# A routing product placed after the token list, and no w_out conversion inside the first routing phase

## The chip, the core and the metric

The kernel runs on one core of one Trainium2 chip. The core has five engines, each with its own in-order instruction queue: PE (matrix products; its weight loads are shown as PEld), DVE (vector work), ACT (scalar activations, copies), POOL (simple vector work and the indexed DMAs) and SP (it issues most DMAs). An engine goes on to its next instruction only when the one in front has what it waits for. The metric is the device time of one execution in microseconds (us).

## What is computed

Three layers follow each other on 3072 tokens with 512 features.

```python
# 1 decayed linear attention, 4 batches x 8 heads x 768 steps x 64
state = gamma * state + k_t v_t^T ;  y_t = scale * q_t state
# 2 mixture of 8 experts: greedy by sorted logits, at most 384 tokens for each expert
logits = x @ w_gate
for (token, e) in order of falling logit: assign if token is free and count[e] < 384
out[tokens of e] = relu(x[tokens of e] @ w1[e]) @ w2[e]
# 3 dense layer
h = x @ w_in ;  out = softplus(h) @ w_out
```

`w_in` and `w_out` arrive as 64-bit floats and are turned into 32-bit ones on the chip with integer work ("conversion").

## The kernel before

**Stages.** The attention stage ends at about 113 us. Then routing finds the first expert and its 384 tokens (the first stage of routing, "phase 0", about 113 to 140 us), with PE kept busy by filler products (`hum`). After that eight experts are worked through, about 107 us each: layer 2 and layer 3 of one expert's tokens, in groups that `plan` lists. For expert i, `m1` and `m2` are the two products of layer 2 for one slice of 128 hidden features, `f1(i,f)` the product with slice f of `w_in` followed by the softplus, `f2(i,f)` the product with slice f of `w_out`, and `xt(i,g)` the transposition of 128 gathered token rows. Operands are split into a high and a low part, so each product is three matmuls. `f1` and `f2` alternate: f1(2), f2(0), f1(3), f2(1), ..., f1(15), f2(13). For expert 0 the three `xt` of expert 1 stand behind f2(9), f2(10) and f2(11).

**What a group gives each engine.** `emit` goes through the list. Before each group `weights` splits the weight slices needed four weighted groups later (ACT writes `whi`, DVE `wlo`). In f1(f) PE writes a PSUM tile `h`, of which there are three in rotation, shared with `m1` and `xt`; ACT makes `sp` from it with three instructions; DVE makes `gf`, which frees the tile; one f1 later ACT makes `gh` and DVE `gl`, which f2(f) needs for its last three matmuls. An `xt` tile is freed by DVE's `xl`.

**Conversion of w_out.** It is cut into 32 pieces and made during expert 0. Each piece takes two steps of `Conv`: a first (DVE, L286, writes `cB`) and a second (DVE, L288, writes `cA`; then POOL adds both, L289, and the next piece's ACT and POOL preparation is issued, POOL at L272 writing that piece's `cA`). So a piece's L288 waits for the POOL instruction L272 which stands behind the POOL addition of the piece before. From the fifth group of expert 0 on the groups do one and two steps by turns, so three in a pair of f1 and f2; and `split_w` first forces the pieces that its slice needs (`late.until`). Eight steps more are done inside phase 0, by `fill` in `start`.

**Routing.** `phase(i)` finds expert i and its tokens while the expert before is worked through. It is a generator; `emit` resumes it after most groups (a "turn"): after every group until the token list exists, after every second one then. In three levels of two comparisons DVE compares keys (`G`), PE counts, DVE decides (`left`, `ind`), PE sums (`upto`), DVE goes on. With the expert known ("expert"), PE and DVE compute positions (`scan`, `ohq` in three parts, `rh`) and twelve small products of `ohq` and `rh` give the token list `ix` ("list"). Then POOL gathers rows by `ix` (`fetch_x`: three indexed DMAs) for the next expert's `xt`. `taken` (14 DVE instructions, L638 to L657) marks the tokens that are gone and makes `rn`; the small product `rn` by `ones` (L606) gives the remaining places, `rem`. In phases 1 to 6 `taken` comes one turn ahead of that product, which stands directly ahead of the list's products; in phase 0 both come behind the list.

Of the kernel before, what the change touches and what calls it, by code (L numbers as in the profile page):

```python
# [52 lines left out]
class Attn:  # L53
# [143 lines left out]
    def hum(self, n):  # L197
        for _ in range(n):
            self.nc.tensor.matmul(self.ph, self.ones, self.ones, start=True, stop=True)
# [123 lines left out]
class Route:  # L323
# [148 lines left out]
        yield  # L472
        self.prepare(slice(c0, c1), 10, 2047, 0.0)

    def phase(self, i, slow=True, hum=lambda n: None, fill=lambda l: None):

        nc, N, E, w = self.nc, self.N, self.E, self.wp
        v = nc.vector
        T = lambda shape, dt, name, **k: w.tile(shape, dt, name=name, **k)
        gap = range  # L480
        last = i == E - 1
# [7 lines left out]
        for l, J in enumerate(() if last else LEVELS):  # L489
            if l:  # L490
                v.tensor_scalar(self.kx, self.bc(self.kp, N, 2), base, S, op0=OP.subtract, op1=OP.mult)
            top = None
            for fine in (0, 1):
                if i or l or fine:
                    thr = self.coarse[J]
                    if fine:
                        thr = T([128, 46], F16, "thr")[:, :J]
                        v.scalar_tensor_tensor(thr, top.to_broadcast([128, J]), J * S, self.jio[:, :J],
                                               op0=OP.mult, op1=OP.add)
                    cuts = (0, N) if slow else (0, N // 2, N - 4, N)  # L500
                    for c0, c1 in zip(cuts, cuts[1:]):
                        self.compare(c0, c1, thr, J, (64 if J > 32 else 32) if i else 46)
                    if l and not fine:
                        v.tensor_scalar(self.kf, self.kp, base, 3000.0 if l == 1 else 1.0, op0=OP.subtract,
                                        op1=OP.min if l == 1 else OP.add)
                    if l == 1 and fine:
                        self.prepare(all, 0, 1023, 4096.0)
                    if i and not l and not fine:
                        self.prepare(all, 10, 2047, 0.0)
                    fill(2 * l + fine)  # L510
                    for _ in gap(2):
                        yield
                ps = self.psum_tile()
                ind = self.ind
                if i:
                    self.count_many(ps, J)
                    self.reached(ps, J)
                else:
                    self.count(ps)
                    v.tensor_tensor(ind, ps[:, 0:E], self.r, op=OP.is_ge)  # L520
                for _ in gap(1 + (i > 1 or i + l > 1)):
                    yield
                f = 4096.0 if fine and l < 2 else 1.0
                nc.tensor.matmul(ps[:, 64:64 + E], self.upto[J, f], ind, start=True, stop=True)
                hum(9 if l == 2 and fine else 6 if fine else 5)
                k = T([128, 1], FT, "ksat", bufs=2)
                v.tensor_reduce(k, ps[:, 64:64 + E], axis=AX.X, op=OP.max)
                if fine:
                    base = T([128, 1], FT, "base")
                    v.scalar_tensor_tensor(base, top, J * f, k, op0=OP.mult, op1=OP.add)  # L530
                top = k
        inc = T([128, E], FT, "inc")
        if last:
# [12 lines left out]
            ps = self.psum_tile()  # L546
# [4 lines left out]
        g2 = T([128, 2, N], BF, "g2")  # L551
# [4 lines left out]
        es = T([128, 1], FT, "es")  # L556
# [23 lines left out]
        pE = pos[:, N:2 * N]  # L580
# [8 lines left out]
        for c0 in range(0, N, h):  # L589
# [3 lines left out]
            if c0 == 0:  # L593
# [2 lines left out]
                                self.cid[:, :, None, :].to_broadcast([128, N, 7, 2]), op=OP.mult)  # L596
                for _ in gap(1):
                    yield
        yield
        if slow:  # L600
            yield
            if not last:
                rn, oh = self.taken(T, pE, inc, g2, es)
            yield
            if not last:
                nc.tensor.matmul(ps[:, 136:136 + E], self.ones, rn, start=True, stop=True)  # L606
        for c in range(0, N, 2):
            nc.tensor.matmul(ps[:, 256:284], q[:, c:c + 2, :].rearrange("p n m -> p (n m)"),
                             rh[:, c:c + 2].rearrange("p n k a -> p (n k a)"), start=c == 0, stop=c == N - 2)
# [10 lines left out]
        yield "list"  # L620
        if last:
            return
        if not slow:
            rn, oh = self.taken(T, pE, inc, g2, es)
            for _ in gap(2):
                yield
            nc.tensor.matmul(ps[:, 136:136 + E], self.ones, rn, start=True, stop=True)
            hum(6)
# [35 lines left out]
class Ffn:  # L664
# [51 lines left out]
    def mm3(self, ps, wh, wl, ah, al, start, stop):  # L716
        nc = self.nc
        nc.tensor.matmul(ps, wh, ah, start=start, stop=False)  # L718
        nc.tensor.matmul(ps, wl, ah, start=False, stop=False)  # L719
        nc.tensor.matmul(ps, wh, al, start=False, stop=stop)  # L720
# [243 lines left out]
    def start(self, ps):  # L964


        hum = lambda n: self.hum(ps, n)
        self.keys = [g[3] for g in self.plan(self.R.E) if g[3]]
        self.loaded = self.done = self.listed = self.phase = 0
        self.gen = None  # L970
        def fill(level):
            for _ in range(2 if level > 1 else 0):
                self.late.step()

        self.late.ahead()
        hum(8)
        for mark in self.R.phase(0, False, hum, fill):
            self.marked(mark, 0)
            if mark == "expert":
                for k in self.keys[:3]:  # L980
                    self.load_raw(k)
                    self.loaded += 1
        self.weights(3)
# [95 lines left out]
```

## Time and profile before

| what | value |
|---|---|
| median of three runs | 1003.72 us (1001.87 to 1003.85) |
| the profiled execution | 1003.05 us, of which the span from first to last instruction is 1001.3 us |
| PE busy | 974.0 us, 97% of the span |
| DVE, ACT, POOL busy | 636.1 us (64%), 582.5 us (58%), 160.0 us (16%) |
| chain of work that ended last | PE 69%, issue 11%, DVE 10%, ACT 4%, DMA 4% of the span |

The span is 1.75 us shorter than the execution that it belongs to; what lies around it is taken as unchanged. PE is busy nearly everywhere, so the time can only change where PE stands still, where its clock is low, or where filler runs. The profile shows PE's granted clock as a share of full speed (1.00 is 2.4 GHz, 0.50 is 1.2 GHz).

### The profile page before, as it was taken

What the parts mean: (1) busy time and instruction counts of PE and PEld (TensorE: products, weight loads), DVE (VectorE), ACT (ScalarE), POOL (GpSimd) and SP (SyncE); (2) the same over time, 40 slices, a digit from 0 to 9 for tenths busy, and PEclk for the clock granted to TensorE, in tenths of its full rate; (3) what the DMA queues carried; (4) which work ended last, traced back from release to release, by engine and by line L of the source; (5) the groups of instructions that cost most, each with busy time, mean ns of one, the idle gap of its engine ahead of it and who ended that gap; (6) DMA issues with size and microseconds to landing.
All of it is one profiled execution on the core that took longest, in us unless ns stands there. A gap on an engine that the chain in (4) does not pass through costs nothing.

```text
span 1001.3 us, 17952 instructions
## 1 busy us (share of the span) xinstructions
PE 974.0 (97%) x6741; PEld 890.8 (89%) x6741; DVE 636.1 (64%) x1638; ACT 582.5 (58%) x1251; POOL 160.0 (16%) x184
## 2 busy tenths in 40 slices
PE   8999899979999999999999999999999999999997
PEld 7888789868998889998998899899989999999996
DVE  6899778787657655755566566655676654454442
ACT  5999525766446653665366645564466546653663
POOL 1655224556100110010101010101010100010001
PEclk9999879989999999999999999999999999999999
DMA  9999345223310123111411041103110340023000
GB/s 361 412 413 386 100 124 163 86 73 116 106 53 32 32 68 103 32 32 27 143 33 32 22 137 43 32 11 118 42 43 1 111 142 1 1 69 101 1 1 32
DMA packets 40599, 95.98 MB, mean 96 GB/s; under 512 B 5312, under 2 KB 5568, under 8 KB 40512
## 3 DMA queue, kind: packets, MB, share of 16 engines
q1 hardware_dynamic: 36528, 82.16, 24.3%
q0 software_dynamic: 3840, 12.59, 3.8%
q8 instruction: 53, 0.87, 0.4%
q14 instruction: 34, 0.28, 0.1%
q10 hardware_dynamic: 144, 0.09, 0.0%
HBM read 82.23 MB, written 12.58 MB: 95 GB/s over the span
## 4 chain that ended last, share of the span: by engine, by line
PE 69%; issue 11%; DVE 10%; ACT 4%; DMA 4%; POOL 1%; SPq 0%; POOLq 0%; ACTq 0%
PE h L726 10%; PE h L727 10%; PE h L729 10%; PE acc L836 6%; PE acc L837 6%; PE acc L841 6%; PE acc L718 4%; PE acc L719 4%; PE acc L720 4%; DMA qk_t<-in_qk_dram 3%; PE pX L184 1%; PE pA L131 1%; DVE gf L802 1%; PE pY L159 1%; PE h L750 1%
## 5 line engine op out<-in xcount | busy, mean ns | idle before, releaser
L802 DVE SCALAR_TENSOR_TENSOR gf<-h,sp 128x384 f32<-128x384 f32 x128 | 71.2, 556 | 171.5 <-ACT sp L793 171.3
L726 PE MATMUL h<-x2h,wih 128*128 128x384 f32 x512 | 176.8, 345 | 0.0
L727 PE MATMUL h<-x2h,wil 128*128 128x384 f32 x512 | 173.4, 339 | 0.0
L836 PE MATMUL acc<-whi,gh 128*128 128x512 f32 x384 | 154.0, 401 | 0.0
L837 PE MATMUL acc<-wlo,gh 128*128 128x512 f32 x384 | 152.0, 396 | 0.0
L791 ACT ACTIVATE sp<-h 128x384 f32<-128x384 f32 x128 | 62.7, 490 | 131.3 <-PE h L729 125.9
L841 PE MATMUL acc<-whi,gl 128*128 128x512 f32 x384 | 111.6, 397 | 0.0
L729 PE MATMUL h<-x2l,wih 128*128 128x384 f32 x512 | 111.0, 338 | 0.0
L710 ACT ACTIVATE h1h<-h 128x384 fp32r<-128x384 f32 x64 | 31.6, 493 | 132.6 <-PE h L729 96.6
L726 PEld LDWEIGHTS h<-x2h,wih 128*128 128x128 f32 x512 | 96.7, 189 | 3.2
L727 PEld LDWEIGHTS h<-x2h,wil 128*128 128x128 f32 x512 | 96.7, 189 | 3.2
L849 POOL DMA_INDIRECT out_dram<-rows,ix x24 | 24.6, 1023 | 438.3 <-ACT rows L847 434.9
L815 ACT ACTIVATE gh<-gf 128x384 fp32r<-128x384 f32 x128 | 67.3, 526 | 45.0 <-DVE gf L802 39.0
L704 DVE TENSOR_TENSOR wlo<-wraw,whi 128x512 fp32r<-128x512 f32 x128 | 86.7, 695 | 9.2 <-ACT whi L703 9.2
L729 PEld LDWEIGHTS h<-x2l,wih 128*128 128x128 f32 x512 | 91.6, 188 | 0.0
L711 DVE SCALAR_TENSOR_TENSOR h1l<-h,h1h 128x384 fp32r<-128x384 f32 x64 | 35.7, 558 | 87.4 <-ACT h1h L710 87.2
L703 ACT ACTIVATE whi<-wraw 128x512 fp32r<-128x512 f32 x128 | 77.3, 626 | 21.0 <-DMA wraw<-in_moe_w_dram 18.3
L704 DVE TENSOR_TENSOR wlo<-wol,whi 128x512 fp32r<-128x512 f32 x128 | 88.6, 698 | 0.9 <-ACT whi L703 0.8
L718 PE MATMUL acc<-h1h,whi 128*128 128x384 f32 x256 | 88.6, 346 | 0.0
L841 PEld LDWEIGHTS acc<-whi,gl 128*128 128x128 f32 x384 | 72.6, 189 | 17.5
L726 PE MATMUL h<-xh,whi 128*128 128x384 f32 x256 | 87.0, 340 | 0.5 <-ACT xh L754 0.5
L719 PE MATMUL acc<-h1h,wlo 128*128 128x384 f32 x256 | 86.3, 337 | 0.0
(197 smaller groups left out, 1931.5 us busy)
## 6 DMA issues: line engine op xcount, KB each, us to landing
wraw<-in_moe_w_dram SPq DMA_DIRECT2D x128, 256.0 KB, 2.8
qk_t<-in_qk_dram SPq DMA_DIRECT2D x24, 512.0 KB, 8.7
kv_t<-in_kv_dram SPq DMA_DIRECT2D x24, 512.0 KB, 8.7
raw<-in_moe_w_in_dram SPq DMA_DIRECT2D x16, 512.0 KB, 8.8
raw<-in_moe_w_out_dram SPq DMA_DIRECT2D x32, 256.0 KB, 2.9
xd<-xs SPq DMA_DIRECT2D x24, 256.0 KB, 7.9
rows<-xd,ix POOLq DMA_INDIRECT x24, 3.6
out_dram<-rows,ix POOLq DMA_INDIRECT x24, 3.7
```

Of the source, the lines that this page charges most:

```text
L703: nc.scalar.activation(hi, raw, AF.Copy)
L704: nc.vector.tensor_tensor(lo, raw, hi.bitcast(FT), op=OP.subtract)
L718: nc.tensor.matmul(ps, wh, ah, start=start, stop=False)
L719: nc.tensor.matmul(ps, wl, ah, start=False, stop=False)
L726: mm(ps, wh(d), ah[:, d], start=d == 0, stop=False)
L727: mm(ps, wl(d), ah[:, d], start=False, stop=False)
L729: mm(ps, wh(d), al[:, d], start=False, stop=d == 3)
L802: self.nc.vector.scalar_tensor_tensor(g, ps, 0.0, a, op0=OP.max, op1=OP.add)
L815: nc.scalar.activation(gh, g, AF.Copy)
L836: nc.tensor.matmul(ps, gh[:, s], wh, start=f == 0, stop=False)
L837: nc.tensor.matmul(ps, gh[:, s], wl, start=False, stop=False)
L841: nc.tensor.matmul(ps, gl[:, s], wh, start=False, stop=f == 15)
```

## The change

In phase 0 no conversion step is done any more: `fill` is gone, and the eight steps (four pieces) are done in expert 0 with the others. The number of steps for each group is as before; where the pieces for a slice are missing, `late.until` forces them.

In phases 1 and 2 `taken` and the product of `rn` move behind the list, with two turns from `taken` to the product, and the list's products stand alone; the number of turns ahead of the list is the same. In phases 3 to 6 (`joined`) the product stays directly ahead of the list's products, but `taken` comes three turns ahead of it, after three turns; the list is three turns later. Phase 1 waits one turn more between the first comparison of the third level and its count. The last phase does none of this.

```diff
-    def phase(self, i, slow=True, hum=lambda n: None, fill=lambda l: None):
+    def phase(self, i, slow=True, hum=lambda n: None):
...
-                    fill(2 * l + fine)
-                    for _ in gap(2):
+                    for _ in gap(2 + (i == 1 and l == 2 and not fine)):
                         yield
...
-        yield
-        if slow:
+        joined = i > 2 and not last
+        for _ in gap(1 + 2 * slow):
             yield
-            if not last:
-                rn, oh = self.taken(T, pE, inc, g2, es)
-            yield
-            if not last:
-                nc.tensor.matmul(ps[:, 136:136 + E], self.ones, rn, start=True, stop=True)
+        if joined:
+            rn, oh = self.taken(T, pE, inc, g2, es)
+            for _ in gap(3):
+                yield
+            nc.tensor.matmul(ps[:, 136:136 + E], self.ones, rn, start=True, stop=True)
...
-        if not slow:
+        if not joined:
             rn, oh = self.taken(T, pE, inc, g2, es)
             for _ in gap(2):
                 yield
...
-        def fill(level):
-            for _ in range(2 if level > 1 else 0):
-                self.late.step()
-
         self.late.ahead()
         hum(8)
-        for mark in self.R.phase(0, False, hum, fill):
+        for mark in self.R.phase(0, False, hum):
```

DVE in phase 0, third comparison, before: `kf` is the last of the comparison's work, `ind` the decision on what PE counted.

```order
L431 TENSOR_TENSOR G<-kx,coarse_81 128x184
L504 TENSOR_SCALAR kf<-kp,base 128x24
L286 SCALAR_TENSOR_TENSOR cB<-raw,cB 128x256
L288 TENSOR_SCALAR cA<-cA 128x256
L520 TENSOR_TENSOR ind<-pS,rem 128x8
L527 TENSOR_REDUCE ksat<-pS 128x1
```

And now:

```order
L431 TENSOR_TENSOR G<-kx,coarse_81 128x184
L504 TENSOR_SCALAR kf<-kp,base 128x24
L519 TENSOR_TENSOR ind<-pS,rem 128x8
L526 TENSOR_REDUCE ksat<-pS 128x1
L498 SCALAR_TENSOR_TENSOR thr<-ksat,jio 128x46
```

The two conversion instructions ahead of the decision are gone, in four places of phase 0.

PE in expert 0, phase 1, before: the `rn` product stands behind f1(9) (L726 to L729), and the list's products behind it.

```order
L727 MATMUL h<-x2h,wil 128x384
L729 MATMUL h<-x2l,wih 128x384 x4
L606 LDWEIGHTS ones
L606 MATMUL rt<-rn,ones 128x8
L608 LDWEIGHTS ohq
L608 MATMUL rt<-rh,ohq 128x28
```

Now the list's products stand behind f2(7), and the `rn` product behind f2(9) and xt(1,0), ahead of f1(12):

```order
L840 MATMUL acc_3004<-whi,gl 128x512
L840 MATMUL acc_3005<-whi,gl 128x512
L840 MATMUL acc_3006<-whi,gl 128x512
L749 MATMUL h<-identp,rows 128x128 x4
L626 LDWEIGHTS ones
L626 MATMUL rt<-rn,ones 128x8
L725 MATMUL h<-x2h,wih 128x384
```

The `rn` product has moved six groups back in PE's queue, the list's products one.

DVE in expert 0 now, from the list (in f2(7)) to the first instructions of `taken` (in f2(8)); `wol` is the converted w_out:

```order
L618 SCALAR_TENSOR_TENSOR ix<-i_3494 128x3
L286 SCALAR_TENSOR_TENSOR cB<-raw,cB 128x256
L703 TENSOR_TENSOR wlo<-wol,whi 128x512
L815 TENSOR_TENSOR gl<-gf,gh 128x384
L801 SCALAR_TENSOR_TENSOR gf<-h,sp 128x384
L288 TENSOR_SCALAR cA<-cA 128x256
L286 SCALAR_TENSOR_TENSOR cB<-raw,cB 128x256
L288 TENSOR_SCALAR cA<-cA 128x256
L637 SCALAR_TENSOR_TENSOR acc<-pos,mem 128x24
L639 TENSOR_TENSOR tin<-oe,inc 128x192
```

and POOL at the same place, with the gather for expert 1:

```order
L289 TENSOR_TENSOR wol<-cA,cB 128x256
L272 TENSOR_SCALAR cA<-cA 128x256
L738 DMA rows<-xd,ix 128x512 x3
L289 TENSOR_TENSOR wol<-cA,cB 128x256
L272 TENSOR_SCALAR cA<-cA 128x256
```

`taken` stands behind the list and behind two second steps (L288); the later of these needs POOL's L272 that stands behind the three gathering DMAs. From f1(7) to f1(11) a pair of f1 and f2 now holds four conversion steps, where it held three.

## Rows read from the trace of the kernel before

**Rows 1.** Waits of PE from 140 us on: total, times, longest (us).

```profile
PE rt L606 <- DVE rn L652: 8.4, 3, 6.8
PE rt L444 <- DVE G L431: 0.6, 1, 0.6
```

**Rows 2.** Windows: PE, PEld, DVE, ACT, POOL busy, PE clock, DMA share, GB/s.

```profile
110.00:140.00 30.00, 24.93 (x268) 22.68 (x265) 23.23 (x108) 7.30 (x16) 10.10 (x12) 0.66 0.37 110
130.00:140.00 10.00, 9.36 (x61) 8.81 (x61) 7.63 (x35) 1.90 (x3) 3.09 (x3) 0.62 0.43 120
215.00:232.00 17.00, 10.22 (x51) 8.97 (x50) 12.95 (x39) 5.89 (x14) 8.99 (x10) 0.70 0.26 82
```

**Rows 3.** Timeline of DVE in phase 0: start, length (us), instruction.

```profile
116.25 0.21 DVE L498 SCALAR_TENSOR_TENSOR thr<-ksat,jio 128x46 f16<-128x46 f32 x1
...
121.02 0.40 DVE L498 SCALAR_TENSOR_TENSOR thr<-ksat,jio 128x46 f16<-128x46 f32 x1
...
122.75 0.42 DVE L286 SCALAR_TENSOR_TENSOR cB<-raw,cB 128x256 int32<-128x256 int32 x1
123.09 0.29 DVE L288 TENSOR_SCALAR cA<-cA 128x256 int32<-128x256 int32 x1
123.29 0.16 DVE L520 TENSOR_TENSOR ind<-pS,rem 128x8 bf16<-128x8 f32 x1
```

**Rows 4.** Timeline of PE: phase 0's filler, ends of f1(6), f1(10), start of f1(14).

```profile
134.66 5.15 PE L962 MATMUL pA<-wih 128*128 128x256 f32 x30
...
203.57 0.87 PE L729 MATMUL h<-x2l,wih 128*128 128x384 f32 x4
...
223.97 0.17 PE L606 MATMUL rt<-rn,ones 128*128 128x8 bf16 x1 [6.78 <-DVE rn L652]
...
230.39 0.87 PE L729 MATMUL h<-x2l,wih 128*128 128x384 f32 x4
...
247.05 0.42 PE L726 MATMUL h<-x2h,wih 128*128 128x384 f32 x1
```

**Rows 5.** Timeline of DVE in expert 0, idle time and releaser in brackets.

```profile
204.21 0.16 DVE L527 TENSOR_REDUCE ksat<-rt 128x1 f32<-128x8 f32 x1
...
206.63 0.68 DVE L704 TENSOR_TENSOR wlo<-wol,whi 128x512 fp32r<-128x512 f32 x1
...
211.03 1.10 DVE L816 TENSOR_TENSOR gl<-gf,gh 128x384 fp32r<-128x384 f32 x1
...
212.84 0.24 DVE L574 TENSOR_TENSOR_SCAN scan<-ones,rt 128x48 f32<-128x48 bf16 x1
...
215.93 1.50 DVE L590 TENSOR_TENSOR ohq<-io,px 128x512 bf16<-128x512 bf16 x2
217.35 0.68 DVE L704 TENSOR_TENSOR wlo<-wol,whi 128x512 fp32r<-128x512 f32 x1
217.95 0.55 DVE L816 TENSOR_TENSOR gl<-gf,gh 128x384 fp32r<-128x384 f32 x1
218.42 0.54 DVE L802 SCALAR_TENSOR_TENSOR gf<-h,sp 128x384 f32<-128x384 f32 x1
...
220.93 0.29 DVE L288 TENSOR_SCALAR cA<-cA 128x256 int32<-128x256 int32 x1 [1.42 <-POOL cA L272]
221.14 0.18 DVE L638 SCALAR_TENSOR_TENSOR acc<-pos,mem 128x24 f32<-128x24 f32 x1
...
224.49 0.69 DVE L704 TENSOR_TENSOR wlo<-wol,whi 128x512 fp32r<-128x512 f32 x1
...
232.94 0.56 DVE L802 SCALAR_TENSOR_TENSOR gf<-h,sp 128x384 f32<-128x384 f32 x1 [3.12 <-ACT sp L793]
```

**Rows 6.** Timeline of POOL: the gather for expert 1 and the conversion behind it.

```profile
230.03 1.05 POOL L739 DMA_INDIRECT rows<-xd,ix  x1 [0.16 <-issue]
...
233.79 0.85 POOL L289 TENSOR_TENSOR wol<-cA,cB 128x256 int32<-128x256 int32 x1 [0.20 <-DVE cA L288]
234.61 0.85 POOL L272 TENSOR_SCALAR cA<-cA 128x256 f32<-128x256 f32 x1
```

## The prediction

> **What bounds the kernel now.** I read the waits of PE first. From 140 us to the tail PE waits for DVE at two kinds of place only: 8.4 us at the `rn` product, in three of its six occurrences, one of them 6.8 us, and 0.6 us once for a comparison `G` [rows 1]. Then the granted clock. The window 110 to 140 us has 0.66; at half speed that is (1 - 0.66) x 30 / 0.5 = 20.4 us at 1.2 GHz, in phase 0. The window 215 to 232 us has 0.70, so 10.2 us at 1.2 GHz, around the long `rn` wait [rows 2]. Everywhere else in the experts PE is busy at 2.4 GHz. So the change can act in phase 0, at the long stop in expert 0, and at the two short stops. The reader should see in [rows 5] why the long stop is there: DVE reaches `taken` at 221.14 and leaves it at 224.49, while PE, at the end of f1(9), has wanted its result since 223.97 - 6.78 = 217.2 [rows 4]. DVE is behind PE by three groups there, and this lag is not made by `taken` alone.
>
> **Phase 0, four pieces of conversion removed.** A first step takes 122.75 to 123.09, 0.34 us to the next start, a second one 0.20 [rows 3]. Four of each are 2.2 us of DVE, the most that can go. Not all of it is on the path: DVE decides on what PE has counted, and mostly the steps fit into PE's count. At 123.29 `ind` did start right behind L288, which I put at 0.35 us late. A small instruction that runs while POOL converts is longer: `thr` 0.40 us at 121.02 against 0.21 at 116.25 [rows 3]; I count five such places at 0.2. So DVE gives `ix` 0.35 + 5 x 0.2 = 1.4 us earlier; the ends are 0 and 2.2.
>
> Behind it PE runs 30 filler matmuls, 134.66 to 139.81 [rows 4], partly at half speed: the window 130 to 140 has 0.62, so the clock rose at about 137.6 [rows 2]. If it rises at the same moment, 1.4 us of earlier start are spent at half speed and give 0.7; if it rises with the filler, all 1.4. I take **-0.8 us**, from 0 to -1.6.
>
> SP, ACT and POOL lose the same four pieces there (four loads, ten ACT copies, the POOL halves); none of them ends last in phase 0, so that is worth nothing more.
>
> A rule bears on the five places. The trace has `thr` 0.19 us longer beside POOL. The Trainium skill, in "SBUF — State Buffer", section "SBUF: two separate sides", says that DVE and GpSimd share one port pair as an exclusive lock, and the later one blocks until the other's instruction is over. By it a hit costs up to the rest of a POOL instruction, and the trace agrees only in part: 0.19 us is less than that. By the rule's extreme the sum here would go to its end of 1.6.
>
> **The two short stops, phases 5 and 6.** 8.4 - 6.8 = 1.6 us [rows 1]. `taken` is 3.35 us of DVE (221.14 to 224.49) [rows 5] and had one turn ahead of the product; now it has three, at least 6 us. Worth **-1.6 us**. The list comes three turns later there, yet five or more groups ahead of the first `xt`; I cost that at nothing, and at up to +1 if DVE meets one of its bursts.
>
> **The long stop, expert 0.** Taking `rn` out of the way saves 6.8 us, and the low clock behind it: PE works again from 223.97, and by 230.39 four matmuls take 0.87 us as at 203.57 [rows 4], so it is at half speed for at most 6.4 us, some 3 lost. That would be -9.8 if DVE could follow. I follow DVE instead, turn by turn, up to the xt(1,1) tile, because f1(14) reuses its PSUM tile and can't start before DVE's `xl`.
>
> Where does DVE last wait for PE in the new order? In f1(6): phase 1's extra turn lets `expert` fall one group later, DVE has less ahead of it, and `gf` must wait for `sp`. PE ends f1(6) at 204.44 before [rows 4]; the 0.6 us for `G` is gone since that count stands one group later, so 203.8. From the end of f1(10), 231.26 [rows 4], to its `gf` at 232.94 [rows 5] are 1.7 us. So `gf` starts at 205.5, on the clock of the trace before (without the gain of phase 0).
>
> From there to the end of `xl` of xt(1,1) DVE has, at start-to-start prices of [rows 3, 5]:
> - 7 `gf` and 6 `gl` at 0.47 (217.95 to 218.42): 6.1
> - 7 `wlo` at 0.60 (217.35 to 217.95) and 2 `xl` of the same size: 5.4
> - 13 first steps at 0.34 and 14 second steps at 0.20: 7.2
> - routing: `expert` 2.42 (204.21 to 206.63), positions 2.55 (212.84 to 215.93 less one second and one first step), the rest of `ohq` 1.42, the list and `rem` some 1.5 (an estimate: eight instructions as short as `taken`'s), `taken` 3.35: 11.2
>
> Together 29.9 us. Then the waits inside DVE's own queue. A second step with little work since the one before waits for POOL: 1.42 at 220.93 [rows 5]. With four steps to a pair this comes in every pair in which no long routing piece stands between; in f2(5), f2(7), f2(9) and f2(10), 4 x 1.42 = 5.7. In f2(8) it is worse. POOL's L272 for that step stands behind the gather, 230.03 to 233.58 with its gaps, then 0.2 idle, L289 and L272 at 0.84 each [rows 6], 5.4 us in all. POOL starts it at about 227; DVE has 2 us of work of its own meanwhile and then stands for 3.7 us, with `taken` behind this wait. Last, instructions that meet POOL's are longer: `gl` 1.10 at 211.03 against 0.55 [rows 5]; half a microsecond in five places, 2.4. Sum: 205.5 + 29.9 + 5.7 + 3.7 + 2.4 = 247.2, against 247.05 when f1(14) starts now [rows 4].
>
> So in this stretch the gain is given back: `rn` is ready at about 235.5, PE stands there some 4.5 us behind xt(1,0), and again for both `xl`. **+0.2 us**; without lengthening beside POOL -2.2, with twice of it +2.6. Behind f1(14) conversion is over and DVE catches up.
>
> **Sum.** -0.8 - 1.6 + 0.2 = -2.2 us. Against the profiled execution, 1003.05, that is 1000.9; against the median of the runs shown, 1003.72, it is **1001.5**. The median lies 0.7 above the profiled one, and I give the forecast against it.
>
> **Rivals.**
> - *DVE follows.* The waits for POOL don't come, or not on the path: up to 5.7 + 3.7 us less on DVE's side. Then PE's own pace sets f1(14). From the end of f1(10) to f1(14) are seven groups and three `xt` in 15.8 us [rows 4], and f1(6) ends eight groups of some 2.1 us earlier: 203.8 + 16.8 + 15.8 = 236.4, even earlier than DVE allows. All of it gives **992**, half of it 997. For it: DVE's 29.9 us of work alone would let PE run on. Against it: in the trace L288 stood for POOL in just this order [rows 5].
> - *Slower: the clock.* PE stands 4.5 us at `rn`; before, 10.2 us at 1.2 GHz came with a stop of 6.8, and 20.4 us in phase 0 [rows 2]. From f1(12) on, a low stretch of L us costs L/2, less some 2.8 us for which PE would stand anyway for the two `xl`. 10.2 us cost 2.3 (1003.8), 20.4 us 7.4 (**1008.9**). It ends slower by over 0.2%, above 1005.7, once L passes 14 us. The Trainium skill ("TensorE: Matmul & The Clock Gate", "What's actually happening") says that half speed is PE's default state and activity releases it; the trace agrees, since the clock came back while PE worked. By the rule the new stop would bring a low stretch again, but one that ends with the work behind it: 1003.8 at most.
> - *No net change.* Phase 0 gives nothing because PE's filler and the gather set its end, and shifted turns in phases 3 to 6 meet new short stops: **1003.5**.
>
> **How the numbers follow.** A measurement of this kernel can tell about 0.2%, 2.0 us, from no change; so faster means below 1001.7 and the forecast lies right at that edge. Forecast 62%, its own range 999.5 to 1003.5, about half of it below the edge; DVE follows 13%; no net change 16%; the clock 9%, most of it slower. Faster 0.33 + 0.13 = 0.46; slower 0.07; same 0.47. The range leaves out most of the first rival and the worst of the second, which are under 2 in 10: 997.0 to 1004.5.
>
> **What would show it.** Right: the wait at L605/L626 in phase 1 still there, some 4 us, now behind xt(1,0) at about 230 to 235; DVE idle some 3.7 us ahead of the L288 in front of `taken`, released by POOL; no wait at the products of `rn` after 600 us; phase 0 shorter by under 1.5 us. Wrong: DVE without waits for POOL between 205 and 245, PE without a stop there, or a second long stretch at 0.50.

## The result, and the profile after

The changed kernel takes 1008.09 us (median of five runs, 1007.67 to 1010.95) where the kernel before takes 1002.69 (1001.87 to 1003.85). The ratio is 1.006, with a 95% interval of 1.0047 to 1.0074: slower by 0.6%, and outside the range of the prediction. The profiled execution has a span of 1006.3 us.

The waits of PE from 140 us on (total, times, longest, in us), which answer to [rows 1]:

```profile
PE acc L835 <- ACT gh L814: 5.1, 3, 1.8
PE rt L626 <- DVE rn L651: 3.2, 1, 3.2
PE h L749 <- DMA rows<-xd,ix: 2.3, 1, 2.3
PE h L725 <- DVE xl L713: 1.3, 2, 1.1
PE acc L840 <- DVE gl L815: 1.0, 1, 1.0
```

Instead of three waits for `rn` there are five kinds of 1 us and more (three others, of 0.5 us each, are left out here), and all five lie in expert 0. The one that leads is new: PE waits for ACT's `gh`. The windows that answer to [rows 2], with one more for the stretch behind (length, then busy time of PE, PEld, DVE, ACT, POOL, granted clock, DMA share, GB/s):

```profile
110.00:140.00 30.00, 25.72 (x272) 24.03 (x273) 21.41 (x104) 3.39 (x6) 3.09 (x3) 0.66 0.27 82
215.00:232.00 17.00, 11.91 (x66) 9.46 (x64) 10.30 (x31) 7.88 (x20) 9.47 (x12) 1.00 0.25 77
232.00:250.00 18.00, 10.38 (x43) 8.77 (x44) 11.45 (x35) 10.17 (x24) 10.65 (x12) 0.81 0.48 153
```

Phase 0 has the same clock as before. In 215 to 232 us the clock is now 1.00, but PE is busy for 11.9 of 17 us, and in 232 to 250 us for 10.4 of 18, with 0.19 x 18 / 0.5 = 6.8 us at 1.2 GHz, some 2.9 of them while PE stands for `rn`. PE in this stretch (start, length, idle time and its releaser), to be read beside [rows 4]:

```profile
237.68 0.66 PE L749 MATMUL h<-identp,rows 128*128 128x128 f32 x4 [2.25 <-DMA rows<-xd,ix]
241.55 0.17 PE L626 MATMUL rt<-rn,ones 128*128 128x8 bf16 x1 [3.21 <-DVE rn L651]
...
254.44 0.45 PE L725 MATMUL h<-x2h,wih 128*128 128x384 f32 x1 [0.24 <-DVE xl L713]
```

The last line is the start of f1(14): 254.44, where it was 247.05, so 7.4 us are lost by then. Expert 0's first product started at 142.97 instead of 143.87, so expert 0 up to f1(14) is 8.3 us longer. Set side by side by the starts of `gf`, expert 1 begins 6.9 us late, and the end of expert 7 is 5.0 us late: some 1.9 us are won in experts 1 to 5. The loss is all in one place, f1(6) to f1(14) of expert 0.

What happens there shows in ACT's waits from 200 to 256 us. Before:

```profile
ACT sp L791 <- PE h L729: 8.6, 7, 4.6
ACT gh L815 <- DVE gf L802: 8.4, 7, 4.0
ACT cA L271 <- POOL wol L289: 1.4, 1, 1.4
```

and DVE's waits there, also before:

```profile
DVE cA L288 <- POOL cA L272: 5.8, 4, 1.4
DVE gf L802 <- ACT sp L793: 5.7, 3, 3.1
```

After, ACT's and then DVE's waits in the same window:

```profile
ACT whi L702 <- POOL wol L289: 22.6, 7, 4.2
DVE cA L288 <- POOL cA L272: 10.1, 6, 2.9
DVE wlo L703 <- ACT whi L702: 5.2, 4, 1.3
DVE gf L801 <- ACT sp L792: 3.2, 5, 0.7
```

Before, ACT waited for PE's products and for `gf`, as an engine does that is off the path, and once, 1.4 us, for POOL. Now it waits for nothing but POOL's converted w_out, seven times, 22.6 us. One turn of this, on ACT, DVE and POOL in this order:

```profile
211.46 0.63 ACT L702 ACTIVATE whi<-wol 128x512 fp32r<-128x512 f32 x1 [3.64 <-POOL wol L289]
212.00 0.51 ACT L814 ACTIVATE gh<-gf 128x384 fp32r<-128x384 f32 x1
...
213.47 0.52 ACT L792 ACTIVATE sp<-sp 128x384 f32<-128x384 f32 x1
...
217.70 0.63 ACT L702 ACTIVATE whi<-wol 128x512 fp32r<-128x512 f32 x1 [2.38 <-POOL wol L289]
```

```profile
206.56 0.56 DVE L801 SCALAR_TENSOR_TENSOR gf<-h,sp 128x384 f32<-128x384 f32 x1 [0.74 <-ACT sp L792]
...
214.03 0.56 DVE L801 SCALAR_TENSOR_TENSOR gf<-h,sp 128x384 f32<-128x384 f32 x1 [0.75 <-ACT sp L792]
214.51 0.28 DVE L288 TENSOR_SCALAR cA<-cA 128x256 int32<-128x256 int32 x1
...
216.56 0.29 DVE L288 TENSOR_SCALAR cA<-cA 128x256 int32<-128x256 int32 x1 [1.44 <-POOL cA L272]
```

```profile
214.87 0.85 POOL L289 TENSOR_TENSOR wol<-cA,cB 128x256 int32<-128x256 int32 x1 [2.63 <-DVE cA L288]
215.69 0.84 POOL L272 TENSOR_SCALAR cA<-cA 128x256 f32<-128x256 f32 x1
216.94 0.72 POOL L289 TENSOR_TENSOR wol<-cA,cB 128x256 int32<-128x256 int32 x1 [0.41 <-DVE cA L288]
```

`whi` ends, `gh` and the three `sp` follow, `gf` has waited for the last of them, L288 stands behind `gf`, POOL adds and prepares, the second L288 has waited for that, POOL adds again, and only then can the next `whi` start. This is a ring: 217.70 - 211.46 = 6.24 us a turn, for one slice of w_out, while PE needs 4.3 us for a pair of f1 and f2 (the starts of f1(6) and f1(7): 201.60 and 205.93). Turns that also hold a piece of routing are longer; the `whi` at 203.99 and the `whi` at 247.29 are six turns apart, 43.3 us, where six pairs are 26. With four pieces of lead less, the split of a slice comes in the very pair that finishes it, and everything behind `whi` on ACT comes to wait for POOL. No engine is busy throughout meanwhile: of the 56 us from 200 to 256, PE is busy for 43.0, DVE for 36.6, ACT for 32.9 and POOL for 31.0.

### The profile page after: what moved, and what is told of

Read it like the earlier page. It is cut to its first block, busy times and chain, and to the rows that moved or that the text cites. A ratio compares the mean times of both kernels' runs of the same rounds, so it can differ in the third digit from the quotient of the medians.

```text
span 1006.3 us, 17961 instructions
## 1 busy us (share of the span) xinstructions
PE 976.6 (97%) x6741; PEld 890.9 (89%) x6741; DVE 636.0 (63%) x1638; ACT 578.9 (58%) x1251; POOL 160.3 (16%) x184
## 4 chain that ended last, share of the span: by engine, by line
PE 68%; issue 11%; POOL 3%; ACT 2%; DVE 1%; DMA 0%; POOLq 0%; ACTq 0%
PE h L725 11%; PE h L728 11%; PE h L726 11%; PE acc L835 7%; PE acc L836 7%; PE acc L840 7%; PE acc L717 4%; PE acc L718 4%; PE acc L719 4%; POOL wol L289 2%; POOL cA L272 1%; PE rt L444 1%; PE h L749 1%; POOL out_dram L848 1%; DMA rows<-xd,ix 0%
## 5 line engine op out<-in xcount | busy, mean ns | idle before, releaser
L726 PE MATMUL h<-x2h,wil 128*128 128x384 f32 x512 | 173.7, 339 | 0.0
L726 PEld LDWEIGHTS h<-x2h,wil 128*128 128x128 f32 x512 | 96.8, 189 | 3.2
L702 ACT ACTIVATE whi<-wol 128x512 fp32r<-128x512 f32 x128 | 78.6, 619 | 28.8 <-POOL wol L289 24.1
L702 ACT ACTIVATE whi<-wraw 128x512 fp32r<-128x512 f32 x128 | 76.6, 624 | 29.2 <-DMA wraw<-in_moe_w_dram 28.8
L835 PEld LDWEIGHTS acc<-whi,gh 128*128 128x128 f32 x384 | 72.3, 188 | 18.3 <-ACT gh L814 7.0
L726 PE MATMUL h<-xh,wlo 128*128 128x384 f32 x256 | 86.3, 337 | 0.0
```

Source lines behind the costliest of these rows:

```text
L702: nc.scalar.activation(hi, raw, AF.Copy)
L726: mm(ps, wl(d), ah[:, d], start=False, stop=False)
L835: nc.tensor.matmul(ps, gh[:, s], wh, start=f == 0, stop=False)
```

## The experiments

All times are medians, with the ratio to the kernel before on the same chip.

**1. Which part of the change costs.** The changed kernel with the eight steps back in phase 0:

```diff
+                    fill(2 * l + fine)
                     for _ in gap(2 + (i == 1 and l == 2 and not fine)):
...
-        for mark in self.R.phase(0, False, hum):
+        for mark in self.R.phase(0, False, hum, fill):
```

> The changed kernel with the eight conversion steps put back into phase 0; the moved `taken` and product stay. Ring theory: the loss of the changed kernel is a ring. From f1(7) on a slice of w_out is finished in the same pair of f1 and f2 in which ACT splits it, so ACT stands at `whi` for POOL's `wol` (22.6 us between 200 and 256 us), `gh` and `sp` stand behind `whi`, `gf` behind `sp`, and the next pair's second step behind `gf`; a turn of this takes 6.2 to 8.0 us where PE needs 4.3 for a pair. With four pieces more in hand no step is forced, ACT doesn't wait for POOL, and f1(14) starts 6 to 11 us earlier than in the kernel before: 992 to 997 us. Move theory: the moved `taken`, behind the list and the gather, is what costs; then the wait for `rn` and the delay stay, and this is no better than 1003 us. My sum for DVE (work plus its waits for POOL) would give about 996 as well, so this run tells only the two parts of the change apart.

999.17 us, ratio 0.9964 (0.995 to 0.9979). The moved routing is a gain of 3.6 us; the removed steps turn it into a loss. It is a smaller gain than expected, since a stop at `rn` stays. ACT's wait for `wol` between 200 and 256 us, PE's longest waits between 200 and 262 us, and the DVE instruction in front of `taken`:

```profile
ACT whi L703 <- POOL wol L289: 1.3, 1, 1.3
```

```profile
PE rt L627 <- DVE rn L652: 3.5, 1, 3.5
PE h L750 <- DMA rows<-xd,ix: 1.0, 1, 1.0
```

```profile
230.75 0.29 DVE L288 TENSOR_SCALAR cA<-cA 128x256 int32<-128x256 int32 x1 [3.69 <-POOL cA L272]
```

**2. The removed steps alone.** The kernel before, without `fill`:

```diff
-        for mark in self.R.phase(0, False, hum, fill):
+        for mark in self.R.phase(0, False, hum):
```

> The kernel before with the eight conversion steps taken out of phase 0 and nothing else; the routing is as before. Ring theory: the forced steps come in f1(7) to f1(12) as in the changed kernel, pairs take 6.2 us and more, ACT waits some 20 us for POOL's `wol`, and the time is 1007 to 1013 us, as slow as the changed kernel or slower. DVE theory (my prediction's sum): eight steps more are 2.2 us of DVE and some waits on POOL, 1004 to 1006 us. Move theory: the routing cost the time, so this is 1002 to 1004 us.

1014.51 us, ratio 1.0116 (1.0099 to 1.0133): above what was expected. The same ring is there, now with `taken` at its old place in front of the list. PE's longest waits between 200 and 262 us, and ACT's between 200 and 256 (the profiled execution took 1012.21 us):

```profile
PE rt L606 <- DVE rn L652: 10.4, 1, 10.4
PE h L726 <- DVE xl L714: 3.5, 1, 3.5
```

```profile
ACT whi L703 <- POOL wol L289: 20.8, 7, 4.1
```

The removal costs 11.8 us with the old routing and, by experiment 1, 8.9 us with the new one. That the moved routing as a whole costs anything is ruled out, and so is my price of some 2 us of DVE and a few waits.

**3. The same steps, split later.** Only the time at which a slice is split changes, and with it the steps that are forced: some five fewer stand ahead of f1(14). All steps stay in expert 0.

```diff
-            self.weights(at[n] + 4)
+            self.weights(at[n] + (2 if 26 <= n < 46 else 4))
```

> The changed kernel, with the splitting of weights two weighted groups ahead instead of four from f1(6) to f1(14) of expert 0. All conversion steps stay in expert 0, the routing is untouched; but a slice's last piece is made two pairs before ACT splits it, and no step is forced up to f2(13) but one at the end. Ring theory: ACT doesn't wait for POOL's `wol`, PE has no waits for `gh`, and f1(14) starts 10 us or more earlier than in the changed kernel: 993 to 999 us. DVE theory: the same work with six steps fewer ahead of f1(14) and the waits of L288 halved, 3 to 4 us earlier: 1004 to 1005 us.

1001.57 us, ratio 0.9993 (0.9984 to 1.0003): 6.5 us less than the changed kernel, more than the 3 to 4 us that a sum on DVE allowed, less than the ring alone promised. f1(14) starts at 245.13, 9.3 us earlier than in the changed kernel. ACT's wait for POOL is down to 6.6 us, and PE's wait for `gh` to 0.9, behind f1(14), where the lookahead goes back to four. What remains is `rn`:

```profile
ACT whi L702 <- POOL wol L289: 6.6, 4, 3.4
```

```profile
PE rt L626 <- DVE rn L651: 4.1, 1, 4.1
PE acc L835 <- ACT gh L814: 0.9, 1, 0.9
```

**4. DVE's wait for POOL taken away.** In the changed kernel a piece is prepared two pieces ahead:

```diff
-    F.late, F.kept = Conv(tc, ctx, 256, halves, 3, 1, (3, 3)), kept
+    F.late, F.kept = Conv(tc, ctx, 256, halves, 3, 2, (4, 3)), kept
```

> The changed kernel with the preparation of a piece (ACT, and POOL L272) issued two pieces ahead instead of one, with one buffer of `cA` more. Then L288 has nothing to wait for on POOL, also behind the gather. DVE theory: the 10.1 us that DVE stands at L288 between 200 and 256 us are the loss; they go, and f1(14) starts some 8 us earlier: 1000 us. Ring theory: POOL still does addition, preparation, addition in this order between a pair's first second step and `whi`, so a turn of the ring loses only the 0.4 us for which POOL waited for L288: six turns, 2.5 us, 1005 to 1007 us, and ACT goes on waiting for `wol`.

1010.06 us, ratio 1.0067 (1.005 to 1.0084), no better than the changed kernel. DVE no longer waits at L288 at all, but it waits 10.9 us at `wlo`, where it was 5.2. So the run tells neither what those 10.1 us cost nor how much the ring does, for it has a fault of its own: with three buffers for raw pieces, preparing earlier leaves less time for the loads, and ACT waits for them.

```profile
ACT cA L271 <- DMA raw<-in_moe_w_out_dram: 10.4, 6, 6.8
```

**5. The ring cut at one link.** In the changed kernel a group's conversion steps stand ahead of `gf`, from f1(6) on; no instruction is added or removed. `gf` also comes behind the routing turn of its group here, since the call that is left for it stands at the end of the group.

```diff
-            if i == 0:
+            if i == 0 and n < 26:
                 self.softplus_sum()
             if i == 0 and n > 3:
```

> The changed kernel with two calls exchanged in `emit` from f1(6) of expert 0 on: the conversion steps of a group now stand ahead of `gf` on DVE, not behind it. Same instructions, same forced steps, same counts. Ring theory: a pair's first L288 no longer waits for `gf`, which waits for `sp`, which stands behind `whi` and `gh` on ACT; it comes behind `gl`. By the rows of the changed kernel a turn is then `whi` 0.63, `gh` 0.41, `gl` 0.5, L288 0.2, POOL 0.85 and 0.82, L288 0.4, POOL 0.85, some 4.9 us in place of 6.2; over six or seven turns 6 to 9 us less, less what the routing stretches and the gather hold anyway: 1000 to 1004 us. If DVE's load and its waits for POOL by themselves are the bound, the order of `gf` and L288 changes nothing: 1007 to 1009 us.

1004.25 us, ratio 1.0019 (1.0008 to 1.0029), some 4 us less than the changed kernel and 0.25 us above the range that was expected. ACT's `whi` in this run:

```profile
210.90 0.63 ACT L702 ACTIVATE whi<-wol 128x512 fp32r<-128x512 f32 x1 [2.74 <-POOL wol L289]
216.15 0.63 ACT L702 ACTIVATE whi<-wol 128x512 fp32r<-128x512 f32 x1 [1.12 <-POOL wol L289]
223.26 0.63 ACT L702 ACTIVATE whi<-wol 128x512 fp32r<-128x512 f32 x1 [3.28 <-POOL wol L289]
228.32 0.63 ACT L702 ACTIVATE whi<-wol 128x512 fp32r<-128x512 f32 x1 [1.22 <-POOL wol L289]
```

The two quiet turns, 210.90 to 216.15 and 223.26 to 228.32, are 5.25 and 5.06 us, where they were 6.24. The links of the expectation add up to 4.7 (it says 4.9); in these two turns POOL's L272 also waited, 0.37 and 0.17 us, for ACT's preparation of the piece (L271), which stands behind `sp`. The turn between, which holds the token positions, is 7.1 (8.0 in the changed kernel). An order on DVE that leaves its instructions as they are is worth some 4 us: what bounds this stretch is the ring, not the amount of work. What the earlier place of the routing turns adds to the 4 us isn't told apart; the two quiet turns show the ring by itself.

**6. The stop at `rn` and the clock.** In the changed kernel the product of `rn` in phase 1 comes two turns later, behind xt(1,1):

```diff
             rn, oh = self.taken(T, pE, inc, g2, es)
-            for _ in gap(2):
+            for _ in gap(2 + 2 * (i == 1)):
                 yield
```

> The changed kernel with the product of `rn` in phase 1 two turns later, behind xt(1,1), so that PE doesn't stand for `rn` behind xt(1,0) (3.2 us, and 6.8 us at 1.2 GHz behind it). Ring theory: the ring sets the pace, and most of the time is taken by the next waits (`gh`, `xl`): 1004 to 1007 us. Clock and stop theory (the stop at `rn` and the low clock behind it are the loss): 3.2 + 3.4 = 6.6 us come back, 1001 to 1002 us.

1009.84 us, ratio 1.0073 (1.0058 to 1.0088). The stop at `rn` is gone, and nothing is won; PE stands even longer at the next thing DVE owes it. PE's waits between 200 and 262 us:

```profile
PE acc L835 <- ACT gh L814: 4.6, 4, 1.8
PE h L725 <- DVE xl L713: 4.2, 1, 4.2
```

So the place where PE stands isn't the cause; the stop is what a late DVE looks like from PE. The run doesn't take the low clock away: behind the new stop PE was at 1.2 GHz again, in all for 6.8 us as in the changed kernel. Experiments 1 and 3 had the same low stretch (0.81 in 232 to 250 us) and took 999.17 and 1001.57 us, so the clock is not what makes the changed kernel slower.

**7. The same with the steps back in phase 0.** Experiments 1 and 6 together.

> The changed kernel with the eight steps back in phase 0 (as in the first run of this study, 999.2 us) and the product of `rn` in phase 1 two turns later. In the first run PE stood 3.5 us for `rn` behind xt(1,0), since `taken` stood behind an L288 that waited 3.7 us for POOL behind the gather, and then ran 6.8 us at 1.2 GHz. Without that stop f1(12) can start at once, and the next wait is that of xt(1,1) for the `gf` of f1(11), some 1.5 us: 3.5 + 3.4 - 1.5 = 5 us less at most, 994 to 997 us. If the wait moves on at full length to the next `gf` and `xl`, 998 to 999.5 us.

999.02 us, ratio 0.9962 (0.995 to 0.9974): the same as experiment 1. The stop of 3.5 us has become two of 1.7 (for `xl`) and 1.6 (for `gl`), as the second case of the expectation had it. The clock in 232 to 250 us was 0.91, so 3.2 us at 1.2 GHz where experiment 1 had 6.8, and the time was the same.

**8. The joined phases alone.** The kernel before, with the new places of `taken` and the list in phases 3 to 6 and nothing else:

```diff
+        joined = i > 2 and not last
+        if joined:
+            for _ in range(2):
+                yield
+            rn, oh = self.taken(T, pE, inc, g2, es)
+            for _ in range(3):
+                yield
+            nc.tensor.matmul(ps[:, 136:136 + E], self.ones, rn, start=True, stop=True)
-        if slow:
+        elif slow:
```

> The kernel before with one part of the change alone: in phases 3 to 6 `taken` comes three turns ahead of the product of `rn` and after three turns, the list three turns later. Conversion and phases 0 to 2 are as before. My prediction's step: the two short stops, 1.6 us, go: 1001 us. No effect, if new stops take their place: 1002.7 us.

1001.12 us, ratio 0.9986 (0.9977 to 0.9995). Of the waits for `rn` only the one of expert 0 is left:

```profile
PE rt L614 <- DVE rn L660: 6.8, 1, 6.8
```

**9. What is left of the stop in experiment 1.** Experiment 1 without conversion steps in f2(8); they come in f1(11) and f2(9).

```diff
-                for _ in range(1 + n % 2):
+                for _ in range({35: 0, 36: 2, 37: 3}.get(n, 1 + n % 2)):
                     self.late.step()
```

> The changed kernel with the eight steps back in phase 0 (999.2 us), and in expert 0 no conversion step in f2(8), where POOL is gathering and `taken` follows on DVE; its two steps come in f1(11) and f2(9). What remained of the stop at `rn` there (3.5 us behind xt(1,0), and 6.8 us at 1.2 GHz behind it) stood behind an L288 that waited 3.7 us for POOL, whose L272 stood behind the three gathering DMAs. If that wait is the cause, `taken` starts 3.9 us earlier, `rn` is ready about when xt(1,0) is done, and 3.5 + 3.4 us come back less a wait of 1 to 2 us for the steps that are made up: 993 to 996 us. If DVE is late there with its own work in any case, the stop moves to the next `gl` and `xl` as it did when the product was moved: 998 to 999.5 us.

997.13 us, ratio 0.9941 (0.9924 to 0.9957), 2 us less than experiment 1 and 1 us short of the better case. PE waits no more for `rn`; there is one stop of 2.2 us for `xl` later. The intervals of the two experiments just overlap; in the traces, from the first `gf` of expert 0 to the first of expert 1, it is 111.9 us for 114.8. The wait of `taken` behind L288 behind the gather, which I had predicted, is real, and it costs 2 to 3 us.

**10. A version that beats both.** Experiment 1, with weights split later as in experiment 3 (two groups ahead, then three), and the steps given out by hand, few of them around routing, two a group behind it:

```diff
+STEPS = {28: 2, 29: 0, 30: 0, 31: 1, 32: 2, 33: 1, 34: 1, 35: 0, 36: 2, 37: 2,
+         39: 2, 40: 2, 42: 2, 43: 2, 45: 2, 46: 2}
...
-            self.weights(at[n] + 4)
+            self.weights(at[n] + (2 if 26 <= n < 39 else 3 if 39 <= n < 48 else 4))
...
-                for _ in range(1 + n % 2):
+                for _ in range(STEPS.get(n, 1 + n % 2)):
```

> The changed kernel with the eight steps back in phase 0, weights split two (later three) weighted groups ahead instead of four from f1(6) of expert 0 on, and the conversion steps given out by a table: none or one in the groups with the token positions, the list and `taken` (f2(5), f1(8), f2(6), f2(8)), two in the groups from f1(11) on. No step is forced, and a slice is complete at least one group before it is split. Eight steps fewer stand ahead of `taken`. If the stops of expert 0 come from steps that meet routing on DVE and the gather on POOL, PE has no wait over 1 us and no low clock there: 991 to 994 us. If the deferred steps make the same stops later, 997 to 999 us.

994.73 us, ratio 0.9921 (0.9904 to 0.9937): 8.0 us less than the kernel before, 0.7 above the better case of the expectation. PE's waits between 200 and 262 us are small, and its clock stays up:

```profile
PE h L728 <- DVE xl L716: 2.2, 2, 1.2
PE acc L843 <- DVE gl L818: 0.2, 1, 0.2
```

```profile
215.00:232.00 17.00, 17.00 (x99) 15.30 (x98) 13.66 (x42) 13.20 (x30) 7.92 (x9) 1.00 0.33 102
232.00:250.00 18.00, 15.52 (x78) 13.26 (x78) 14.93 (x41) 11.37 (x27) 10.09 (x11) 1.00 0.30 94
```

In 215 to 232 us PE is busy throughout, where it was for 10.2 of 17 us in [rows 2].

## Why the prediction was wrong

**The step that failed** is "I follow DVE instead, turn by turn". I summed DVE's own work and its waits for POOL, and took it that behind the `gf` of f1(6) DVE would never again wait for ACT. Between 200 and 256 us it waited 8.4 us for ACT: 5.2 at `wlo` and 3.2 at `gf`, the first 2.0 of them at that `gf` and the `wlo` ahead of it. Put into my sum this is nearly the whole error: 247.2, less 0.9 for the earlier start, plus 8.4, plus 0.7 because the waits at L288 came to 10.1 in place of 9.4, is 255.4; f1(14) started at 254.44. The waits that I listed were there nearly at their size (at L288 five of 1.4 us for four, and 2.9 us ahead of `taken` for 3.7, where 5.4 less 2 is 3.4), DVE's own work was 1.0 us less than I had summed, and the waits that I left out decided.

Why I left them out: the trace of before has none at `wlo` between 200 and 256 us; there ACT never stood at `whi` for a slice that wasn't whole. I had written down that the number of steps forced by `until` rises, and counted them as 0.5 us of DVE for a first and a second one. I didn't ask who stands behind an instruction that needs what is being forced. On ACT that is `gh`, `sp`, and the preparation of the pieces that follow, so ACT was a link and not a bystander. In the turn shown above `gh` starts at 212.00, while its `gf` had ended at 206.56 + 0.56 = 207.1: 4.9 us behind its input, because it stood behind `whi` (and, for the first 0.7, behind the preparation of two pieces). The Trainium skill says in "PSUM — Partial Sum Buffer", section "Engine vs sequencer instructions", that the queues of ScalarE, VectorE and GpSimd are strict FIFO; the trace agrees by these 4.9 us.

**Point by point.**
- *The long stop, expert 0*: +0.2 predicted, +8.3 measured, of which experiment 3 gives back 6.5 us by splitting later and experiment 5 some 4 by one exchange on DVE.
- *The two short stops*: -1.6 predicted. Right: experiment 8 gives 1.7 us (1002.78 to 1001.12; 0.5 to 2.3 by its interval), and no cost of the later list shows there.
- *Phase 0*: -0.8 predicted, and expert 0's first product is 0.9 earlier, but that is luck. Phase 0's first comparison `G` ran at 114.88 us in the trace of before and at 114.19 to 114.39 in all the others, so some 0.7 of the 0.9 lies ahead of phase 0. From that `G` on, `ix` comes after 19.7 to 19.9 us in the six traces without the steps and after 20.5 to 20.9 in the six with them: 0.9 us earlier, where I had 1.4. Of this hardly anything is left at expert 0's first product: 28.7 to 29.0 us from `G` without the steps (30.7 in experiment 4), 28.8 to 29.1 with them (29.6 in experiment 9). On this the rival *No net change* had the size right; what sets the end of phase 0 was not varied.
- *DVE follows*: by its time the rival came near only where the steps went back to phase 0, in part (999.17) and more once the steps were spread (994.73, beside the 992 that it gave). By its mechanism it didn't: in both DVE went on waiting at L288 for POOL, 6.1 and 6.5 us between 200 and 256 us.
- *Slower: the clock*: the result was slower, but not by this. The new stop at `rn` was 3.2 us, the stretch at 1.2 GHz 6.8 us, below the 14 us from which it would decide, and 3.4 us shorter than in the kernel before. The 10.2 us that I put behind the stop were also too many: some 4.3 of them had passed while PE stood, and of the 6.8 now 2.9. (The expectations of experiments 6, 7 and 9 have the same fault, with 3.4 us for about 2 to 2.7.) Experiments 1 and 3, with the same low stretch, were 8.9 and 6.5 us faster.
- *What would show it*: the wait at `rn` behind xt(1,0) (3.2 us for 4), DVE's idle time ahead of `taken` (2.9 us for 3.7), no waits for `rn` behind 600 us and the small gain in phase 0 all came, and the time was still wrong. One sign did point at it: the wait at `rn` came at 238.3 to 241.6 us, where I had said about 230 to 235. Otherwise every item tested what I had counted, and none the assumption that nothing else was late. Waits at `wlo`, `gf` or `whi` should have been on the list.

**What stays open**: the sizes of the links in turns with routing, which I read off the trace and didn't vary, and what DVE's 10.1 us at L288 cost by themselves, since experiment 4 put another wait in their place.

## What to carry to other kernels

When a change eats the lead of a producer, don't add up one engine: start at the instruction that needs the product, list what stands behind it in that engine's queue, and follow it until the chain closes on the producer; if it closes, the time of one turn is the bound, here 6.2 us against 4.3. Lead can be won on the consumer's side, with no work made faster (split later, 6.5 us). And put on the list of signs at least one that would show an engine late which the sum takes to be early.

## What the runs showed of the hardware

The clock was kinder than I had allowed for. Around stops of PE of 3.2 us (changed kernel), 3.5 us (experiment 1) and 4.2 us (experiment 6) there were some 6.8 us at 1.2 GHz, where a stop of 6.8 us had 10.2 [rows 2]. In these four the clock fell while PE stood and came back while it worked. Only the part behind the stop slows PE: by windows cut at the end of the stop it was 5.9 us before, 3.9 in the changed kernel and in experiment 6, and 5.3 in experiment 1. Shorter stops had a low stretch too: 3.2 us in 232 to 250 us (0.91) in experiment 7, with stops of 1.6 and 1.7 us, and in experiment 9, with one of 2.2 us; there the clock fell only after PE had begun to work again (at 238.85 and 237.10 us). In experiment 10, with two stops of at most 1.2 us, the window of 232 to 250 us shows 1.00.

Three gathers of 128 rows (L738) held POOL's queue in the changed kernel from 232.91 to 236.89 us, 4.0 us, and the conversion behind them waited; that is where DVE's 2.9 us ahead of `taken` come from.
